# Retention, experts and a rational FFN in one program: moved row splits, output subtractions and first-group placement

## Chip, cores and metric

One core of one Trainium2 chip runs the whole program. The metric is the device time of one execution in microseconds (us); the figure for the kernel before is the median of three runs.

## What is computed

Three blocks follow each other, all in float32 precision. The first is attention with a decaying state, for 2 batches of 8 heads, 768 steps, head size 64. The second sends each of the 1536 tokens to one of 8 experts, in the order in which they come. The third is a feed-forward block with a rational function in the middle.

```python
state = gamma * state + k_t v_t^T;  y_t = scale * q_t state     # per head
logits = x @ w_gate;  expert_idx = argmax(logits);  gate_w = its softmax
h = relu(disp @ w1[e]);  y = h @ w2[e];  out = gate_w * y       # per expert
h = x @ w_in;  g = P(h) / (Q(h) + 1e-6);  return g @ w_out      # P, Q polynomials
```

## The kernel before

**Two parts for each float32 number.** TensorE (PE) multiplies in a rounded float32 format. So weights and activations are split into a rounded high part and a remainder, the low part, and a product is three matmuls: high by high, high by low, low by high. ScalarE (ACT) writes the high part (`whi`, `xh`, `yh`, ...) by a copy. VectorE (DVE) writes the low one by a subtraction (`wlo`, `xl`, `yl`, ...). Weights come in halves of 128 by 1024, six halves ahead of their use; `prep_next` (L169) loads one, splits the next one due, and stands once in every group of matmuls.

**Attention** goes over 12 units of 128 tokens. Of a unit, `scores` multiplies keys and queries, `mask` masks them on DVE, `inter` multiplies the state with the queries, `intra` adds the masked scores' products with the values, `attn_xt` scales the result on DVE, and `gate_mm` multiplies it with the gate weights of the experts one unit later. The values are first scaled by powers of gamma: by GpSimd (POOL) in `scale` (L275), up to unit 9. After units 0 to 6 (the first group) and 7 to 11 (the second) the tokens' places in the experts are worked out on DVE (`gate_parts`, `rank_pos`, `rank_put`, `gate_put`). In unit 10, `place_first` (L535) has PE add up the first group's places, DVE turns them into row indices, and POOL fetches by an indirect DMA the rows of expert 0's first 128 tokens into `xg0`. Those rows are transposed by PE in `early_x`, just after unit 11.

**Experts.** Expert 0 is done in two pieces, the first in the tail of attention, the second in `first_expert`, whose last result `y0` is transposed in expert 1 by `y_turn` (L848). Experts 1 to 7 run one loop (`moe`, L978). An expert has 224 token slots. Its up-projection is four groups (`fp`) of 24 matmuls into one of three PSUM banks `e1`; ACT takes the relu's high part `h` (L1006), DVE its remainder (L1007), and a weight half is split. In groups 1 and 3 `expert_x` (L963) transposes 128 or 96 rows of the next expert on PE and splits them into `xh` (ACT, L974) and `xl` (DVE, L975). All the transposed rows go through one PSUM bank, `xt`, so the next transposes wait for the `xl` before. Its down-projection is four quarters (`q`) of 16 matmuls into two PSUM tiles `acc[0]` and `acc[1]`, each the only buffer of its name. Of its four blocks `o` of 128 output columns, 0 and 1 go to `acc[0]`, 2 and 3 to `acc[1]`, and both tiles are written from the first quarter on: the order of the first matmuls is two pairs to `acc[0]`, then `acc[1]`.

At an expert's end `y_high` (L860) takes the high parts `yh` from both tiles on ACT, and `y_low` (L863) makes the remainders on DVE, two subtractions for each tile:

```python
tt(out=yl.bitcast(F32), in0=acc[:, :, 0], in1=yh.bitcast(F32), op=ALU.subtract)
tt(out=yl, in0=acc[:, :, 1], in1=yl.bitcast(F32), op=ALU.add)
```

**Beside this**, `dec_slot` decodes the feed-forward block's weights, which come as 64-bit numbers: in every third group or quarter two steps on ACT (L197, L198), in the next one two on DVE (L205, L206) and an addition on POOL (L209), then a store.

**What sets the order.** The program is written in the order in which each engine takes its instructions; nothing is moved by a scheduler. Each engine has its own queue and waits, by semaphores, for the others.

Of the kernel before, what the change touches and what calls it, by code (L numbers as in the profile page):

```python
# [21 lines left out]
E = 8  # L22
# [62 lines left out]
class Build:  # L85
# [528 lines left out]
    def attention(self):  # L614
        nc, tc, a = self.nc, self.tc, self.a
        with ExitStack() as st:
            self.ap = self.pool("attn", stack=st)
            self.pa = self.pool("pa", space=PSUM, stack=st)
            self.kv, self.sc, self.scm, self.s, self.yt, self.xt = {}, {}, {}, {}, {}, {}
            self.route, self.place, self.xk, self.rk, self.where = {}, {}, {}, {}, {}  # L620
            self.qd, self.yp = {}, {}
            n0, n1 = self.cols["ident"][0], self.cols["tri"][0]
            nk = self.cols["gk"][0]
            self.c0 = self.ap.tile([128, -(-(nk + H * D) // 32) * 32], F32, name="c0")[:, 0 : nk + H * D]
            self.ca = self.ap.tile([128, -(-(n0 - nk) // 32) * 32], F32, name="ca")[:, 0 : n0 - nk]
            self.wi = self.ap.tile([128, 4, 256], F32, name="wi")[:, :, 0:136]
            self.tri = self.ap.tile([128, 128], BF16, name="tri")
            self.ones = self.ap.tile([128, 128], BF16, name="ones")
            self.lgs = self.ap.tile([128, NU, 4, E], F32, name="lgs")
            self.xg0 = self.ap.tile([128, DM], F32, name="xg0")  # L630
            self.x0 = [self.ap.tile([128, 4, 128], F32R, name=n) for n in ("xh0", "xl0")]
            self.wu = self.ap.tile([128, 128], BF16, name="wu")
            self.attn_load(0, 0)
            nc.sync.dma_start(out=self.c0, in_=a["c0"])
            self.attn_load(1, 0)
            self.attn_part(0, 3)
            self.attn_load(1, 1)
            self.attn_load(2, 0)
            nc.sync.dma_start(out=self.ca[:, 0 : n1 - nk], in_=a["ct"][:, nk:n1])
            nc.sync.dma_start(out=self.ct, in_=a["ct"][:, n0:])  # L640
            self.attn_load(2, 1)
            for c in range(2):
                self.attn_load(3, c)
            nc.sync.dma_start(out=self.ca[:, n1 - nk :], in_=a["ct"][:, n1:n0])
            dve, pool = nc.vector, nc.gpsimd
            dve.memset(self.wu, 0.0)
            dve.memset(self.ones, 1.0)
            self.warm(WA)
            self.scores(0)
            self.mask_first()  # L650
            for h in (0, 4):
                self.scale(0, pool, slice(h, h + 4))
            self.y_table(0, pool)
            self.scale(1, pool)
            self.y_table(1, pool)
            self.warm(WC)
            ident = self.col("ident").unsqueeze(1).to_broadcast([128, 4, 128])
            wg = self.col("wg").rearrange("p (k e) -> p k e", e=E)
            done = {GROUPS[b + 1] - 1: b for b in range(len(GROUPS) - 1)}
            for u in range(NU):  # L660
                last = u == NU - 1
                if u + 4 < NU:
                    for c in range(2):
                        self.attn_load(u + 4, c)
                self.load_next(LOADS[u])
                if u + 2 < UA + 3:
                    self.scale(u + 2, pool)
                if u + 2 < UPB:
                    self.y_table(u + 2, pool)
                for n in LO_AT.get(u, ()):  # L670
                    self.split_lo(n // 2, n % 2)
                if 3 < u < NU - 1:
                    self.scores(u + 1)
                    self.mask(u + 1)
                if u - 2 in done:
                    next(gate)
                self.inter(u)
                if u - 4 in done:
                    self.place_first()
                if u == 3:  # L680
                    self.scores(u + 1)
                    self.mask(u + 1)
                self.intra(u)
                if u:
                    self.attn_xt(u)
                if u - 2 in done:
                    next(gate)
                if u:
                    self.state(u)
                if u < 3:  # L690
                    self.scores(u + 1)
                    self.mask(u + 1, 1 if u else 2)
                if u == 0:
                    self.state(u)
                if u == 0:
                    self.attn_xt(0)
                    nc.scalar.activation(out=self.wi[:, :, 0:128], in_=ident, func=AF.Copy)
                    nc.scalar.activation(out=self.wi[:, :, 128:], in_=wg, func=AF.Copy)
                if u == 3:
                    nc.scalar.activation(out=self.tri, in_=self.col("tri"), func=AF.Copy)  # L700
                    nc.scalar.activation(out=self.b0a, in_=self.ab[:, 4:5], func=AF.Abs)
                    nc.scalar.activation(out=self.b1a, in_=self.ab[:, 5:6], func=AF.Abs)
                    nc.vector.memset(self.cq, 1.0 + 1e-6)
                if u:
                    self.gate_mm(u - 1)
                if u - 2 in done and not last:
                    self.rank_mm(done[u - 2])
                if 0 < u < NU - 1:
                    self.gate_out(u - 1, (0,))
                for n in LO_MID.get(u, ()):  # L710
                    self.split_lo(n // 2, n % 2)
                if u - 1 in done:
                    gate = self.gate_parts(done[u - 1])
                    next(gate)
                if 0 < u < NU - 1:
                    self.gate_out(u - 1, (1,))
                if UA + 3 <= u + 2 < NU:
                    self.scale_heads(u + 2)
                for n in HI_AT.get(u, ()):
                    self.split_hi(n // 2, n % 2)  # L720
                if u - 2 in done and not last:
                    self.rank_pos(done[u - 2])
                if u - 3 in done and not last:
                    self.rank_put(done[u - 3])
                    self.gate_put(done[u - 3])
                for n in LO_END.get(u, ()):
                    self.split_lo(n // 2, n % 2)
            self.attn_tail()
# [250 lines left out]
    def moe(self):  # L979
        nc = self.nc  # L980
        with ExitStack() as st:
# [5 lines left out]
            mp = self.mp  # L987
            self.xh, self.xl = {}, {}
            self.first_expert()
            for e in range(1, E):  # L990
                xh, xl = (t.pop(e)[:, :, 0:W] for t in (self.xh, self.xl))
                h = {}
                for fp in range(4):
# [3 lines left out]
                    for fi in range(2):  # L997
# [9 lines left out]
                    nc.vector.scalar_tensor_tensor(  # L1007
                        out=hl, in0=ps, scalar=0.0, in1=hh.bitcast(F32), op0=ALU.max, op1=ALU.subtract
                    )
                    self.prep_next()  # L1010
                    if fp == 2 and e + 1 < E:
                        self.x_gate(e + 1, 1)
                    if fp % 2 and e + 1 < E:
                        self.expert_x(e + 1, fp // 2)
                        if e + 2 < E:
                            self.gather(2 * (e + 2) + fp // 2)
                    self.dec_slot(8 * e + fp)
# [4 lines left out]
                for q in range(4):  # L1022
# [14 lines left out]
                    if q == 3:  # L1037
                        at = bass.ds(self.start(e), W)
                        y = [(acc[i], slice(2 * i, 2 * i + 2), at) for i in range(2)]
                        for t in y:  # L1040
                            self.y_high(*t)
                            if e < E - 1:
                                self.y_low(*t)
                    if (e, q) == (1, 0):
                        self.y_turn(self.y0, 1)
                    if q == 2 and e + 2 < E:
                        self.x_gate(e + 2, 0)
# [375 lines left out]
```

## Time and profile before

| | |
|---|---|
| median of 3 runs | 507.47 us (507.04 to 509.14) |
| the profiled execution | 507.05 us |
| its span, first to last instruction | 505.3 us |
| PE busy | 494.8 us |
| DVE busy | 413.3 us |
| ACT busy | 365.9 us |
| POOL busy | 242.7 us |

The span runs from the first instruction of the program to the last. Attention takes about the first 55 us of it, the experts go on to about 246 us, and the feed-forward block takes the rest. Matmuls are pipelined: a row's duration is longer than the distance from its start to the next one's. A row of the timeline gives start, duration, engine, line, operation and tiles; the time in brackets is the engine's idle time before it and what ended that.

### The profile page before, as it was taken

The page shows a single profiled execution, that of the slowest core. Times are in us where ns is not written, and L with a number is a line of the kernel's source. Part 1 is how long each engine was busy: PE and PEld are TensorE (multiplying, and loading weights), DVE is VectorE, ACT ScalarE, POOL GpSimd, SP SyncE. Part 2 cuts the span into 40 slices and gives each one's busy share as a digit, 9 for nine tenths or more (in the row PEclk, how much of TensorE's full clock was granted, in tenths as well). Part 3 has the DMA queues.
Part 4 walks back from the last instruction along what each step waited for, and adds up shares of the span by engine and source line. Part 5 has one row for each costly group of instructions (what it writes and reads, how often), then busy time and mean ns, then how long its engine had stood idle before and what let it go on. Part 6 is the DMA issues. An engine that isn't in the chain of part 4 may idle for free.

```text
span 505.3 us, 9192 instructions
## 1 busy us (share of the span) xinstructions
PE 494.8 (98%) x3401; PEld 430.2 (85%) x3401; DVE 413.3 (82%) x602; ACT 365.9 (72%) x605; POOL 242.7 (48%) x187
## 2 busy tenths in 40 slices
PE   8999999999999999999999999999999999999995
PEld 5898878899999999898888888888888888888883
DVE  2579858789998987995696989999899998865973
ACT  1356639768677686755788989989999987767760
POOL 2621041033244734353464456767478774454774
PEclk9999999999999999999999999999999999999998
DMA  8999676898997999982400011312124000000203
GB/s 303 409 414 399 207 230 206 346 322 275 299 344 252 366 260 304 288 266 74 167 0 2 1 42 43 109 57 86 42 62 129 19 1 0 2 1 0 84 21 146
DMA packets 27265, 83.07 MB, mean 164 GB/s; under 512 B 4944, under 2 KB 5200, under 8 KB 27216
## 3 DMA queue, kind: packets, MB, share of 16 engines
q1 hardware_dynamic: 24160, 73.52, 42.4%
q0 software_dynamic: 2624, 7.35, 4.2%
q10 hardware_dynamic: 432, 1.57, 0.9%
q8 instruction: 27, 0.44, 0.3%
q14 instruction: 22, 0.18, 0.1%
HBM read 71.94 MB, written 10.49 MB: 163 GB/s over the span
## 4 chain that ended last, share of the span: by engine, by line
PE 64%; DVE 2%; issue 1%; ACT 1%; POOL 1%; POOLq 0%; DVEq 0%
PE h L1127 9%; PE h L1125 9%; PE h L1126 9%; PE acc L373 8%; PE o L1198 8%; PE o L1196 8%; PE o L1197 8%; PE e L1001 3%; PE e L1002 2%; PE e L1003 2%; POOL out L1227 1%; PE tp L971 0%; DVE wlo L154 0%; DVE fw L1162 0%; DVE fx L1164 0%
## 5 line engine op out<-in xcount | busy, mean ns | idle before, releaser
L154 DVE TENSOR_TENSOR wlo<-raw,whi 128x1024 fp32r<-128x1024 f32 x80 | 112.2, 1415 | 15.0 <-ACT whi L149 14.5
L1176 POOL TENSOR_TENSOR gg<-fx,gg 128x512 fp32r<-128x512 f32 x47 | 61.1, 1299 | 69.9 <-issue 62.1
L149 ACT ACTIVATE whi<-raw 128x1024 fp32r<-128x1024 f32 x80 | 83.5, 1054 | 1.8 <-PE acc L373 1.6
L1125 PE MATMUL h<-yh,whi 128*128 128x512 f32 x192 | 74.8, 390 | 0.0
L1196 PE MATMUL o<-whi,gg 128*128 128x512 f32 x192 | 74.8, 390 | 0.0
L1127 PE MATMUL h<-yh,wlo 128*128 128x512 f32 x192 | 74.8, 390 | 0.0
L1197 PE MATMUL o<-wlo,gg 128*128 128x512 f32 x192 | 74.7, 389 | 0.0
L1126 PE MATMUL h<-yl,whi 128*128 128x512 f32 x192 | 74.7, 389 | 0.0
L1198 PE MATMUL o<-whi,gg 128*128 128x512 f32 x192 | 74.7, 389 | 0.0
L373 PE MATMUL acc<-h,whi 128*128 128x448 f32 x224 | 71.4, 377 | 0.0
L1151 POOL TENSOR_TENSOR fw<-fh,fw 128x512 f32<-128x512 f32 x48 | 64.3, 1339 | 13.5 <-ACT fw L1140 12.8
L209 POOL TENSOR_TENSOR gq<-gq 128x512 int32<-128x512 int32 x16 | 26.1, 1628 | 86.0 <-DVE gq L206 47.9
L1138 ACT ACTIVATE fx<-h,ct 128x512 f32<-128x512 f32 x48 | 37.2, 776 | 37.6 <-PE h L1127 37.5
L1001 PE MATMUL e<-xh,whi 128*128 128x224 f32 x224 | 62.0, 277 | 0.1
L1002 PE MATMUL e<-xl,whi 128*128 128x224 f32 x224 | 61.5, 274 | 0.0
L1003 PE MATMUL e<-xh,wlo 128*128 128x224 f32 x224 | 61.5, 274 | 0.0
L373 PE MATMUL acc<-h,wlo 128*128 128x224 f32 x224 | 59.0, 263 | 0.0
L373 PEld LDWEIGHTS acc<-h,whi 128*128 128x128 f32 x224 | 42.0, 187 | 3.2
L1001 PEld LDWEIGHTS e<-xh,whi 128*128 128x128 f32 x224 | 43.0, 192 | 0.5 <-ACT yh L861 0.4
L1002 PEld LDWEIGHTS e<-xl,whi 128*128 128x128 f32 x224 | 43.0, 192 | 0.0
L1003 PEld LDWEIGHTS e<-xh,wlo 128*128 128x128 f32 x224 | 43.0, 192 | 0.0
L373 PEld LDWEIGHTS acc<-h,wlo 128*128 128x128 f32 x224 | 42.7, 191 | 0.1
(167 smaller groups left out, 1096.3 us busy)
## 6 DMA issues: line engine op xcount, KB each, us to landing
raw<-wm SPq DMA_DIRECT2D x61, 512.0 KB, 7.2
r<-wf SPq DMA_DIRECT2D x32, 512.0 KB, 4.9
kv<-kv SPq DMA_DIRECT2D x23, 512.0 KB, 8.5
wd<-gq SPq DMA_DIRECT2D x16, 256.0 KB, 6.6
raw<-wd SPq DMA_DIRECT2D x8, 512.0 KB, 6.7
xd<-xs SPq DMA_DIRECT2D x12, 256.0 KB, 7.1
raw<-wm ACTq DMA_DIRECT2D x3, 512.0 KB, 6.2
c<-c SPq DMA_DIRECT2D x1, 348.0 KB, 3.7
```

The costliest lines, as they stand in the source:

```text
L149: nc.scalar.activation(out=self.whi[i][:, sl], in_=raw, func=AF.Copy)
L154: (eng or self.nc.vector).tensor_tensor(out=self.wlo[i][:, sl], in0=raw, in1=self.whi[i][:, sl].bitcast(F32), op=ALU.subtract)
L373: self.nc.tensor.matmul(out, lhsT=w, rhs=x, start=start, stop=stop, skip_group_check=True)
L1001: nc.tensor.matmul(ps[:, fi], lhsT=wh[:, sl], rhs=xh[:, k], start=(k == 0), stop=False)
L1002: nc.tensor.matmul(ps[:, fi], lhsT=wh[:, sl], rhs=xl[:, k], start=False, stop=False)
L1003: nc.tensor.matmul(ps[:, fi], lhsT=wl[:, sl], rhs=xh[:, k], start=False, stop=(k == 3))
L1125: nc.tensor.matmul(h, lhsT=wh[:, sl], rhs=self.yh[:, k, ts], start=(k == 0), stop=False)
L1126: nc.tensor.matmul(h, lhsT=wh[:, sl], rhs=self.yl[:, k, ts], start=False, stop=False)
L1127: nc.tensor.matmul(h, lhsT=wl[:, sl], rhs=self.yh[:, k, ts], start=False, stop=(k == 3))
L1196: self.nc.tensor.matmul(ps, lhsT=gh[:, ms], rhs=wh[:, ws], start=first, stop=False)
L1197: self.nc.tensor.matmul(ps, lhsT=gh[:, ms], rhs=wl[:, ws], start=False, stop=False)
L1198: self.nc.tensor.matmul(ps, lhsT=gl[:, ms], rhs=wh[:, ws], start=False, stop=last)
```

## The change

Four places change in the order of the program; no arithmetic does.

- The scaling of unit 1's values on POOL is done in two halves of four heads.
- `place_first` in unit 10 stands behind `intra` and `attn_xt` of that unit, and no longer ahead of them.
- In groups 1 and 3 of an expert, `expert_x` stands ahead of the group's weight half. POOL's `gather` of the rows for the expert after next stays behind it.
- The `y_low` of an expert's two tiles stand in the next expert, one in group 0 and one in group 2, each behind that group's weight half. For expert 7 they stay at the end. `y_turn` of expert 0's last rows comes after the second quarter of expert 1's down-projection, and no longer after the first.

```diff
--- before.py
+++ after.py
@@ -651,7 +651,8 @@
             for h in (0, 4):
                 self.scale(0, pool, slice(h, h + 4))
             self.y_table(0, pool)
-            self.scale(1, pool)
+            for h in (0, 4):
+                self.scale(1, pool, slice(h, h + 4))
             self.y_table(1, pool)
             self.warm(WC)
             ident = self.col("ident").unsqueeze(1).to_broadcast([128, 4, 128])
@@ -675,14 +676,14 @@
                 if u - 2 in done:
                     next(gate)
                 self.inter(u)
-                if u - 4 in done:
-                    self.place_first()
                 if u == 3:
                     self.scores(u + 1)
                     self.mask(u + 1)
                 self.intra(u)
                 if u:
                     self.attn_xt(u)
+                if u - 4 in done:
+                    self.place_first()
                 if u - 2 in done:
                     next(gate)
                 if u:
@@ -987,6 +988,7 @@
             mp = self.mp
             self.xh, self.xl = {}, {}
             self.first_expert()
+            y = []
             for e in range(1, E):
                 xh, xl = (t.pop(e)[:, :, 0:W] for t in (self.xh, self.xl))
                 h = {}
@@ -1007,11 +1009,14 @@
                     nc.vector.scalar_tensor_tensor(
                         out=hl, in0=ps, scalar=0.0, in1=hh.bitcast(F32), op0=ALU.max, op1=ALU.subtract
                     )
+                    if fp % 2 and e + 1 < E:
+                        self.expert_x(e + 1, fp // 2)
                     self.prep_next()
                     if fp == 2 and e + 1 < E:
                         self.x_gate(e + 1, 1)
+                    if fp % 2 == 0 and y:
+                        self.y_low(*y.pop(0))
                     if fp % 2 and e + 1 < E:
-                        self.expert_x(e + 1, fp // 2)
                         if e + 2 < E:
                             self.gather(2 * (e + 2) + fp // 2)
                     self.dec_slot(8 * e + fp)
@@ -1039,9 +1044,7 @@
                         y = [(acc[i], slice(2 * i, 2 * i + 2), at) for i in range(2)]
                         for t in y:
                             self.y_high(*t)
-                            if e < E - 1:
-                                self.y_low(*t)
-                    if (e, q) == (1, 0):
+                    if (e, q) == (1, 1):
                         self.y_turn(self.y0, 1)
                     if q == 2 and e + 2 < E:
                         self.x_gate(e + 2, 0)
```

On DVE, between the down-projection of expert 1 and the second group of expert 2, there stood (`yl` are the subtractions of `y_low`, each with a register instruction, ISA; `h` a group's remainder; `wlo` a weight half):

```order
L870 TENSOR_LOAD st_83
L865 ISA
L865 TENSOR_TENSOR yl<-acc,yh 128x2x224
L866 ISA
L866 TENSOR_TENSOR yl<-acc,yl 128x2x224
L865 ISA
L865 TENSOR_TENSOR yl<-acc,yh 128x2x224
L866 ISA
L866 TENSOR_TENSOR yl<-acc,yl 128x2x224
L1007 SCALAR_TENSOR_TENSOR h<-e_1614,h 128x2x224
L154 TENSOR_TENSOR wlo<-raw,whi 128x1024
L1007 SCALAR_TENSOR_TENSOR h<-e_1652,h 128x2x224
```

and with the change, over the same place:

```order
L871 TENSOR_LOAD st_83
L1009 SCALAR_TENSOR_TENSOR h<-e_1611,h 128x2x224
L154 TENSOR_TENSOR wlo<-raw,whi 128x1024
L866 ISA
L866 TENSOR_TENSOR yl<-acc,yh 128x2x224
L867 ISA
L867 TENSOR_TENSOR yl<-acc,yl 128x2x224
L1009 SCALAR_TENSOR_TENSOR h<-e_1651,h 128x2x224
```

The four subtractions ahead of the first remainder are gone; the first two stand behind the first weight half.

On DVE, from the remainder of group 1 of expert 2 to that of group 3 (`xl` the next expert's rows; `gq` the decoder), there stood:

```order
L1007 SCALAR_TENSOR_TENSOR h<-e_1652,h 128x2x224
L154 TENSOR_TENSOR wlo<-raw,whi 128x1024
L975 TENSOR_TENSOR xl<-tp,xh 128x4x128
L205 TENSOR_SCALAR gq<-gq 128x512
L206 SCALAR_TENSOR_TENSOR gq<-r_1530,gq 128x512
L1007 SCALAR_TENSOR_TENSOR h<-e_1700,h 128x2x224
L154 TENSOR_TENSOR wlo<-raw,whi 128x1024
L1007 SCALAR_TENSOR_TENSOR h<-e_1737,h 128x2x224
L154 TENSOR_TENSOR wlo<-raw,whi 128x1024
```

and with the change:

```order
L1009 SCALAR_TENSOR_TENSOR h<-e_1651,h 128x2x224
L976 TENSOR_TENSOR xl<-tp,xh 128x4x128
L154 TENSOR_TENSOR wlo<-raw,whi 128x1024
L205 TENSOR_SCALAR gq<-gq 128x512
L206 SCALAR_TENSOR_TENSOR gq<-r_1520,gq 128x512
L1009 SCALAR_TENSOR_TENSOR h<-e_1699,h 128x2x224
L154 TENSOR_TENSOR wlo<-raw,whi 128x1024
L866 ISA
L866 TENSOR_TENSOR yl<-acc,yh 128x2x224
L867 ISA
L867 TENSOR_TENSOR yl<-acc,yl 128x2x224
L1009 SCALAR_TENSOR_TENSOR h<-e_1738,h 128x2x224
```

The rows' `xl` moved ahead of the weight half, and the other two subtractions came in behind group 2's weight half, ahead of group 3's remainder.

On PE, in unit 10 (`yt<-kv,s` is `inter`, `yt<-scm,kv` is `intra`, `tp` and `L540` are the place matmuls):

```order
 L373 MATMUL sc<-kv 128x128 x8
 L373 MATMUL yt<-kv,s 64x128 x8
+L373 MATMUL yt<-scm,kv 64x128 x8
 L533 MATMUL tp<-rr,pe 128x96 x7
 L540 LDWEIGHTS ones
 L540 MATMUL tp<-run,ones 128x1
-L373 MATMUL yt<-scm,kv 64x128 x8
 L373 MATMUL st<-kv 64x64 x8
 L373 MATMUL xk<-wi,xt 64x136 x8
```

The unit's value products moved ahead of the place matmuls.

## Rows read from the trace of the kernel before

**Rows 1.** The page: its first line, and the busy time of the engines (share of the span).
```profile
span 505.3 us, 9192 instructions
...
PE 494.8 (98%) x3401; PEld 430.2 (85%) x3401; DVE 413.3 (82%) x602; ACT 365.9 (72%) x605; POOL 242.7 (48%) x187
```

**Rows 2.** Waits of PE over the whole span: us in total, times, longest.
```profile
PE ytp L852 <- DVE xl L975: 1.1, 1, 1.1
...
PE tp L971 <- DVE xl L975: 0.9, 1, 0.9
...
PE tp L533 <- DVE rr L527: 0.3, 1, 0.3
...
PE yt L373 <- POOL kv L278: 0.3, 1, 0.3
```

**Rows 3.** Expert 5 as one stretch: us, busy per engine, PEclk, DMA share, GB/s.
```profile
172.19:193.80 21.61, 21.61 (x170) 21.14 (x169) 19.11 (x23) 13.95 (x21) 12.18 (x9) 1.00 1.02 296
```

**Rows 4.** Timeline of POOL in unit 1: start us, us, what, [idle before it].
```profile
9.82 1.04 POOL L278 TENSOR_TENSOR kv<-kv,c 128x512 f32<-128x512 f32 x1 [3.69 <-DMA kv<-kv]
```

**Rows 5.** Timeline of DVE in unit 10, same columns.
```profile
50.94 0.69 DVE L381 TENSOR_TENSOR xt<-yt,qd 128x512 f32<-128x512 f32 x1 [0.21 <-PE yt L373]
```

**Rows 6.** POOL's gather in unit 10: its timeline row, and its time to landing by source line.
```profile
50.34 1.20 POOL L921 DMA_INDIRECT xg<-xd,gidx  x1 [10.59 <-DVE tab L544]
...
DMA to landing us min/median/max: 3.6/3.6/3.6
```

**Rows 7.** Timeline of PE: first-group transposes; first matmuls into `acc[1]`, experts 2, 4, 5, 7.
```profile
54.76 0.44 PE L735 MATMUL xtp<-ct,xg 128*128 128x128 f32 x2
...
119.17 0.38 PE L373 MATMUL acc<-h,whi 128*128 128x448 f32 x1
...
162.78 0.38 PE L373 MATMUL acc<-h,whi 128*128 128x448 f32 x1
...
184.40 0.37 PE L373 MATMUL acc<-h,whi 128*128 128x448 f32 x1
...
227.82 0.37 PE L373 MATMUL acc<-h,whi 128*128 128x448 f32 x1
```

**Rows 8.** Timeline of DVE in expert 2.
```profile
107.10 0.62 DVE L865 TENSOR_TENSOR yl<-acc,yh 128x448 f32 x1 [0.35 <-ACT yh L861]
...
110.41 0.62 DVE L1007 SCALAR_TENSOR_TENSOR h<-e,h 128x448 fp32r<-128x448 f32 x1 [0.84 <-ACT h L1006]
...
111.36 1.22 DVE L154 TENSOR_TENSOR wlo<-raw,whi 128x1024 fp32r<-128x1024 f32 x1 [0.33 <-ACT whi L149]
...
114.04 1.23 DVE L154 TENSOR_TENSOR wlo<-raw,whi 128x1024 fp32r<-128x1024 f32 x1 [0.32 <-ACT whi L149]
...
115.18 0.68 DVE L975 TENSOR_TENSOR xl<-tp,xh 128x512 fp32r<-128x512 f32 x1
...
115.78 0.42 DVE L205 TENSOR_SCALAR gq<-gq 128x512 int32<-128x512 int32 x1
...
116.23 0.69 DVE L206 SCALAR_TENSOR_TENSOR gq<-r,gq 128x512 int32<-128x512 int32 x1
...
116.84 0.62 DVE L1007 SCALAR_TENSOR_TENSOR h<-e,h 128x448 fp32r<-128x448 f32 x1
...
117.37 2.16 DVE L154 TENSOR_TENSOR wlo<-raw,whi 128x1024 fp32r<-128x1024 f32 x1
```

**Rows 9.** Timeline of POOL in expert 2.
```profile
117.16 1.28 POOL L209 TENSOR_TENSOR gq<-gq 128x512 int32<-128x512 int32 x1 [8.10 <-ACT whi L149]
```

**Rows 10.** Timeline of DVE in experts 4 and 5.
```profile
154.42 0.62 DVE L1007 SCALAR_TENSOR_TENSOR h<-e,h 128x448 fp32r<-128x448 f32 x1 [1.20 <-ACT h L1006]
...
182.62 2.15 DVE L154 TENSOR_TENSOR wlo<-raw,whi 128x1024 fp32r<-128x1024 f32 x1
```

**Rows 11.** Timeline of ScalarE (ACT) in experts 2 and 7.
```profile
116.06 1.05 ACT L149 ACTIVATE whi<-raw 128x1024 fp32r<-128x1024 f32 x1
...
219.88 0.54 ACT L1006 ACTIVATE h<-e 128x448 fp32r<-128x448 f32 x1
```


## Prediction

> **What bounds the kernel now.** I read the page's busy times first, then the waits of TensorE (PE), then its trace stage by stage, and last VectorE's (DVE's) order in the expert stage. PE is busy 494.8 us of a span of 505.3 [rows 1], and the view of its waits lists little between start and tail [rows 2]: 1.1 us for the transposes of `y_turn`, 0.9 us for a set of transposes in `expert_x`, 0.3 us for the place matmuls of unit 10, 0.3 us for GpSimd's (POOL's) scaling of unit 1. So PE bounds the kernel, and an edit counts only by what it takes from PE's waits or adds to them. DVE is the engine to watch. In expert 5 it is busy 19.11 us of 21.61, at a granted clock of 1.00 [rows 3], and its queue is in order: what is put ahead of an instruction that PE needs makes it late by its whole length.
>
> **Attention, the two small edits.** The scaling of unit 1 takes 1.04 us in one piece [rows 4]. In two halves the first is ready after about 0.5, heads 0 to 3 can start without PE's 0.3 us of waiting, and the second half is ready about when PE gets to it. I take 0.3 us; the ends are 0 (the next thing is late by as much) and 0.4.
>
> Placing the first group behind unit 10's value products removes PE's other wait of 0.3 us. But three things now stand later: the place matmuls, behind the products; the index computation on DVE, behind `attn_xt(10)` (0.69 us) where it was ahead of it [rows 5]; and the gather on POOL, issued at 50.34, which lands 3.6 us after its issue [rows 6] and whose rows PE transposes at 54.76 [rows 7]. So they landed some 0.8 us before PE used them. PE now comes 0.3 us sooner and the rows about 0.6 later, and the margin is used up. I take nothing; the ends are a gain of 0.3 and a loss of 0.3.
>
> **Experts, what is removed.** `y_turn` comes a quarter later, and `expert_x` ahead of the weight half, so that `xl` is not behind a subtraction of 1.2 us: PE's wait of 1.1 us goes. In expert 6 the transposes waited 0.9 us [rows 2] for an `xl` that stood behind the four subtractions of `y_low` at the expert's start; that goes too. Together 2.0 us.
>
> **Experts, what is added.** `y_low` reads the down-projection's accumulators, two PSUM tiles with one buffer each. Until now all four of its subtractions ran right after an expert's last matmul, half an expert before PE wrote these tiles again. Now the second pair, that of `acc[1]`, stands behind the third up group's remainder **and** its weight half. PE's fifth matmul of the down-projection writes `acc[1]` and must wait for that pair, and all of PE's queue behind it. The wait is new, in experts 2 to 7.
>
> I walk expert 2 with the starts of DVE's rows [rows 8], PE's times kept. A row's successor starts about 0.08 before its end (114.04 + 1.23, then 115.18). The weight half of group 0 starts at 111.36. Behind it, at 112.50, goes the first `y_low` pair, twice 0.62, so 1.20 to the next start. Then group 1's remainder (0.62) is at 113.70, `xl` at 114.24, its weight half at 114.84, the decoder's two steps at 115.98 and 116.43, group 2's remainder at 117.04. The decoder's POOL addition starts 0.24 after the second step ends (116.92, then 117.16) and takes 1.28 [rows 9]. In the trace the weight half behind it starts at 117.37, takes 2.16 and ends 1.09 after POOL; alone it takes 1.22. So here POOL runs from 117.36 to 118.64, the half ends at 119.73, and the second pair, 1.28 long, at 120.93. PE wants `acc[1]` at 119.17 [rows 7]. **Wait: 1.8 us.**
>
> The others by the same steps:
> - Expert 5 has the decoder in the same place: 1.8. In the trace its third weight half runs from 182.62 to 184.77 [rows 10], already past PE's 184.40, before any `y_low` is put behind it.
> - Expert 3 has no decoder step ahead. The weight half waits for its high part from ScalarE, which in expert 2's times ends at 117.11 [rows 11]: half 117.15 to 118.37, pair to 119.57, wait 0.45 with the signal. This is the least that any of experts 2 to 6 can have.
> - Expert 4 has the decoder after the first pair. From group 0's remainder at 154.42 [rows 10], with 0.95 to its half as at 110.41 to 111.36: pair 156.51, decoder 157.71, remainder 158.77, `xl` 159.31, POOL 159.09 to 160.37, half to 161.46, group 2's half 161.92 to 163.14, second pair to 164.34, against 162.78: 1.6.
> - Expert 6 has the decoder ahead of group 0, where POOL delays the first half by about a microsecond: 1.2, between 0.8 and 1.5 by when ScalarE has the decoder's input.
> - Expert 7 has shorter up groups and no transposes. ScalarE frees group 0 at 220.42 [rows 11]: remainder 220.45, half 221.40, pair 222.54, decoder 223.74, remainder 224.80, POOL to 226.40, half to 227.49, next half to 229.17, pair to 230.37, against 227.82: 2.6, taken as 2.4 since that ScalarE step moves up a little.
>
> Sum 1.8 + 0.45 + 1.6 + 1.8 + 1.2 + 2.4 = 9.25. DVE's own work does not grow, and behind the wait it has room again: the last group's remainder is needed only when three quarters of the down-projection are done, and `xl` only at the next expert. So I cost what is queued behind the second pair at nothing; were that cover gone, the next expert's first group would wait.
>
> **A rule beside it.** The row shows that a weight half started beside POOL's addition takes 2.16 instead of 1.22. The Trainium skill (SBUF — State Buffer, Who interferes with whom) says that a DVE instruction with two SBUF inputs and a GpSimd instruction that reads SBUF exclude each other, and that issue order decides which waits. By that rule, the trace agrees (2.16 against 1.22), and the price falls on DVE wherever a step that reads PSUM stands between decoder and half; were POOL the one to wait, the time would be the second rival's.
>
> **Sum.** 507.05 (the profiled run: span 505.3 and 1.75 around it) + 9.25 − 2.0 − 0.3 = 514.0. The median of the runs is 0.42 above the profiled one, less than my terms are sure to.
>
> **Rivals.**
> - *The second pair is in time* (faster): PE never waits on `acc[1]`, and 507.05 − 2.3 = 504.75. It decides in expert 2 at 119.17: DVE must have ended the third half by 117.9. For it: none of DVE's work grew. Against: ScalarE alone ends that half's high part at 117.11, and the half takes 1.22. 5%.
> - *The halves win against POOL*: where the decoder is near, a wait is shorter by up to 0.94: 0.9, 0.45, 1.3, 0.9, 0.5, 1.5, sum 5.55, so 507.05 + 5.55 − 2.3 = 510.3. For it: a few tenths decide which starts first. Against: rows 8, where POOL did, with the same order. 20%.
> - *It balances*: all six waits as small as expert 3's, 2.7 against 2.3: 507.45. Rows 10 speak against it (expert 5). 9%.
> - *It piles up*: a late decoder step holds up loads and ScalarE, every expert pays 0.6 more, and the gather is late too: 507.05 + 12.85 − 2.0 = 517.9. 14%.
>
> **Numbers.** The forecast itself has 52%. The range is 509.8 to 517.5: from just under the second rival to just under the last. A measurement tells about 0.5% (2.5 us) from no change. Slower by more: forecast, second and last rival, 86%; within: 9%; faster: 5%.
>
> **What would show it.** PE's waits must list `acc` waiting for DVE's `yl` (the second subtraction), six times, longest in expert 7, 7 to 11 us in all; `ytp` and `tp` waiting for `xl` must be gone, and the wait for POOL's `kv` nearly so. If `xtp` waits for the gather, the margin was smaller than read. The prediction is wrong if no `acc` waits for `yl`, or if the sum of these waits is under 5 us.

## The result and the profile after

The changed kernel takes 513.89 us (median of 4 runs, 513.38 to 515.21), the kernel before 507.62 beside it. The ratio is 1.0123, 95% interval 1.0093 to 1.0152: slower by 1.2%. The forecast was 514.0, range 509.8 to 517.5. The profiled execution took 514.13 us; the figures below compare it with the profiled 507.05 of before.

The changed kernel's page, its first line and its busy times, which answer to [rows 1]:

```profile
span 512.3 us, 9187 instructions
...
PE 496.0 (97%) x3401; PEld 429.7 (84%) x3401; DVE 409.3 (80%) x602; ACT 366.5 (72%) x605; POOL 242.4 (47%) x188
```

PE's busy time grew by 1.2 us (its rows' modelled ends) and the span by 7.0. DVE works no longer than before; PE stands still for longer. Its waits over the span, which answer to [rows 2] (us in total, times, longest):

```profile
PE acc L373 <- DVE yl L867: 6.7, 6, 1.9
PE sc L373 <- DMA kv<-kv: 1.1, 1, 1.1
PE wp L302 <- DVE wu L646: 1.0, 1, 1.0
PE yt L373 <- ACT s L344: 0.5, 1, 0.5
PE xtp L736 <- DMA xg<-xd,gidx: 0.5, 1, 0.5
```

The waits of `ytp` and `tp` for `xl`, those for `rr` and for POOL's `kv` are gone. A new one stands at the top: `acc` for the second subtraction of `y_low`, six times. Three of the six on PE's timeline, with the rows around the first (start us, us, engine, line, operation; in brackets the idle time before and what ended it):

```profile
118.59 0.38 PE L373 MATMUL acc<-h,whi 128*128 128x448 f32 x1
118.81 0.27 PE L373 MATMUL acc<-h,wlo 128*128 128x224 f32 x1
119.75 0.47 PE L373 MATMUL acc<-h,whi 128*128 128x448 f32 x1 [0.68 <-DVE yl L867]
120.06 0.26 PE L373 MATMUL acc<-h,wlo 128*128 128x224 f32 x1
120.16 0.38 PE L373 MATMUL acc<-h,whi 128*128 128x448 f32 x1
...
166.03 0.47 PE L373 MATMUL acc<-h,whi 128*128 128x448 f32 x1 [1.85 <-DVE yl L867]
...
234.71 0.47 PE L373 MATMUL acc<-h,whi 128*128 128x448 f32 x1 [1.92 <-DVE yl L867]
```

These are the first matmuls into `acc[1]`, as in [rows 7]. A wait costs more than its bracket says. Between the starts of 118.81 and 119.75 lie 0.94 us where 0.10 is usual, as from 120.06 to 120.16; and the first matmul behind the wait takes 0.31 to the next start, where another takes 0.21 or 0.22. That is 0.94 in all for a bracket of 0.68. PE's weight loads (PEld) show it too: the load of the matmul at 120.16 started 0.10 ahead of it, at 120.06, but that of the matmul behind the wait only together with it:

```profile
119.75 0.19 PEld L373 LDWEIGHTS acc<-h,whi 128*128 128x128 f32 x1 [0.96 <-DVE yl L867]
120.06 0.19 PEld L373 LDWEIGHTS acc<-h,whi 128*128 128x128 f32 x1
```

So the time is counted by the starts of the experts' first matmuls in the two traces. The row of expert 7 ends at the first matmul of the feed-forward block, which comes behind the first quarter of that expert's down-projection:

| stretch | before, us | after, us | difference | bracket of `acc` | forecast |
|---|---|---|---|---|---|
| start to expert 1 | 83.67 | 84.72 | +1.05 | | -0.3 |
| expert 1 | 23.28 | 21.97 | -1.31 | | -1.1 |
| expert 2 | 21.61 | 22.56 | +0.95 | 0.68 | +1.8 |
| expert 3 | 21.94 | 22.49 | +0.55 | 0.30 | +0.45 |
| expert 4 | 21.69 | 23.79 | +2.10 | 1.85 | +1.6 |
| expert 5 | 21.61 | 23.56 | +1.95 | 1.67 | +1.8 |
| expert 6 | 22.67 | 22.19 | -0.48 | 0.30 | +1.2 - 0.9 |
| expert 7 | 13.23 | 15.41 | +2.18 | 1.92 | +2.4 |
| the rest | 275.58 | 275.64 | +0.06 | | 0 |

The waits add 8.28 (expert 6's wait of before was worth 1.03 by distance), the removed ones give 2.34 (1.31 and 1.03), the start takes 1.05; with 0.06 that is 7.05. Between the medians the loss is 6.3.

### The profile page after: what moved, and what is told of

Its sections match the earlier page's. It is cut to its first block, busy times and chain, and to the rows that moved or that the text cites. A ratio compares the mean times of both kernels' runs of the same rounds, so it can differ in the third digit from the quotient of the medians.

```text
span 512.3 us, 9187 instructions
## 1 busy us (share of the span) xinstructions
PE 496.0 (97%) x3401; PEld 429.7 (84%) x3401; DVE 409.3 (80%) x602; ACT 366.5 (72%) x605; POOL 242.4 (47%) x188
## 4 chain that ended last, share of the span: by engine, by line
PE 57%; DVE 6%; issue 3%; ACT 2%; POOL 1%; POOLq 0%; DVEq 0%; ACTq 0%
PE h L1128 9%; PE h L1130 9%; PE h L1129 8%; PE acc L373 8%; PE o L1199 7%; PE o L1201 7%; PE o L1200 7%; DVE wlo L154 2%; ACT whi L149 1%; DVE yl L866 1%; POOL out L1230 1%; DVE yl L867 1%; DVE h L1009 1%; PE e L1005 1%; PE e L1004 1%
## 5 line engine op out<-in xcount | busy, mean ns | idle before, releaser
L154 DVE TENSOR_TENSOR wlo<-raw,whi 128x1024 fp32r<-128x1024 f32 x80 | 107.9, 1363 | 13.3 <-ACT whi L149 13.0
```

The costliest lines, as they stand in the source:

```text
L154: (eng or self.nc.vector).tensor_tensor(out=self.wlo[i][:, sl], in0=raw, in1=self.whi[i][:, sl].bitcast(F32), op=ALU.subtract)
```

## The experiments

The letters stand for the theories named in the expectations. "W" is the forecast's: `acc[1]` has one buffer, its second pair of subtractions comes too late, and PE waits. All ratios are to the kernel before, run beside them.

**Is the late pair the loss?** First all four subtractions go back to the expert's end; the other moves stay (`low_end`):

```diff
-                    if fp % 2 == 0 and y:
-                        self.y_low(*y.pop(0))
...
                             self.y_high(*t)
+                            if e < E - 1:
+                                self.y_low(*t)
```

> The changed kernel with one part undone: all four subtractions of y_low stand at the expert's end again; the other moves stay. Theory W (PE waits for acc[1]'s late pair, and that is the whole loss): no matmul of acc waits for yl, and the distance that the six waits added, 8.3 us by the starts of experts 2 to 7 in the changed kernel's trace, goes: 513.9 - 8.3 = 505.6 us, between 505 and 506.5. Rival O (the loss lies in the other moves: xl ahead of the weight half, or the first group's placement): the time stays above 510.

Measured: 505.47 us, ratio 0.9966 (0.9949 to 0.9984). No matmul of `acc` waits. The whole loss goes, and what is left of the change is a gain of 0.3%. O, that the other moves cost the time, is out.

Then the kernel before with that move alone (`low_only`).

> The kernel before with one part of the change alone: y_low in groups 0 and 2 of the next expert, each behind the weight half. W: six waits of acc for yl come back, the wait of expert 6's transposes (1.0 by distance) goes, that of y_turn (1.3) stays: 507.6 + 8.3 - 1.0 = 514.9 us, between 513.5 and 516. O: within 2.5 us of the kernel before, 507.6.

Measured: 517.45 us, ratio 1.0194 (1.0158 to 1.023), 2.5 us more than expected and above the range. The six waits are there (7.3 us), but two experts take longer than in the changed kernel: expert 2 by 0.94, as its wait is 1.61 and not 0.68 (the race behind this is told under the attention edits), and expert 4 by 2.28, with 26.07 us. The table by stretches shows why expert 4 does (us, then busy us of PE, its weight loads, DVE, ACT, POOL, each with a count, then the granted clock, DMA share, GB/s):

```profile
164.00:167.00 3.00, 1.96 (x15) 1.50 (x13) 3.00 (x5) 3.00 (x7) 2.70 (x2) 1.00 0.99 270
167.00:168.30 1.30, 0.00 (x0) 0.00 (x1) 1.27 (x4) 1.30 (x3) 0.92 (x1) 1.00 0.87 251
168.30:170.00 1.70, 1.70 (x6) 1.57 (x7) 1.70 (x3) 0.64 (x1) 0.00 (x0) 0.55 0.98 375
170.00:171.60 1.60, 1.60 (x7) 1.51 (x6) 1.57 (x4) 0.26 (x1) 0.00 (x0) 0.50 1.05 428
171.60:174.00 2.40, 2.40 (x16) 2.25 (x16) 2.40 (x2) 1.01 (x2) 2.17 (x2) 0.94 0.97 362
```

PE stood still for 0.83 us before the transposes at 165.53 and for 1.51 before `acc[1]` at 168.30. Right behind the second stop the granted clock is 0.50, the lower of its two levels, for more than 3 us. In that stretch the first matmul of a pair takes 0.40 to the next start, not 0.21:

```profile
170.09 0.60 PE L373 MATMUL acc<-h,whi 128*128 128x448 f32 x1
170.49 0.39 PE L373 MATMUL acc<-h,wlo 128*128 128x224 f32 x1
```

Of the 2.28 us the transposes' wait is 0.83, the shorter `acc` wait -0.34, and the 1.8 that are left go with the lower clock. The mechanism is W's; the clock is a price that W had left out.

Third, DVE's order stays as changed and PE's demand is moved (`acc_late`): in the first two quarters the matmuls into `acc[0]` come first, then those into `acc[1]`.

```diff
-                    for f in range(2 * q, 2 * q + 2):
+                    fs, os = (range(4), range(2 * q, 2 * q + 2)) if q < 2 else (range(2 * q, 2 * q + 2), range(4))
+                    for f in fs:
                         x = h[f // 2][:, f % 2]
-                        for o in range(4):
+                        for o in os:
```

> The changed kernel, DVE's order untouched, with PE's demand moved instead: the first two quarters of a down-projection do all their matmuls into acc[0] first (eight pairs), then those into acc[1], so that acc[1] is first written 6 pairs of 0.315 us, 1.9 us, later. W (the single buffer of acc[1] is what PE waits for): the six waits, at most 1.92 us, shrink to 0.1 or nothing: 513.9 - 8.3 = 505.6 us, between 505 and 507. Rival D (DVE is too slow as a whole in these experts, and PE waits for it wherever it stands): a new wait of a similar size further on in the same expert, 510 or more.

Measured: 506.82 us, ratio 0.9986 (0.9971 to 1.0002), 1.2 above the expectation and within its range. With the subtractions in the same place, the loss goes: what counts is when PE wants the buffer. PE's waits:

```profile
PE tp L972 <- ACT xg L962: 0.8, 1, 0.8
PE acc L373 <- DVE yl L867: 0.7, 1, 0.7
PE xtp L736 <- DMA xg<-xd,gidx: 0.7, 1, 0.7
```

Five of the six waits are gone. The one of 0.7 is expert 4's, where DVE's first remainder comes 5.1 us behind the expert's first matmul (154.29 and 149.20; 4.3 in the changed kernel's expert 4, 156.08 and 151.74). The wait of `tp` is no heir of `acc`'s: `xl` is ready, ACT's scaling of the rows (`x_gate`) is late (see below). So D, that DVE is too slow wherever PE waits for it, is out but for expert 4.

The changed kernel was run a second time beside these (`again`).

> The changed kernel once more, beside the others: 513.9 us, between 513 and 514.8; acc waiting for yl six times, 6 to 8 us in all, longest in experts 4, 5 and 7 (1.6 to 2.0 each), shorter in 2, and 0.3 in 3 and 6. The place where it may differ is expert 2, where POOL's addition and the third weight half start within 0.2 us of each other: 0.7 with the half first, up to 1.7 with POOL first.

Measured: 513.46 us, ratio 1.0125 (1.0099 to 1.015). The waits repeat: 0.68, 0.30, 1.80, 1.69, 0.30, 1.92.

**Where may the second pair stand?** In group 2, but ahead of the weight half (`pair_first`):

```diff
+                    if fp == 2 and y:
+                        self.y_low(*y.pop(0))
                     self.prep_next()
...
-                    if fp % 2 == 0 and y:
+                    if fp == 0 and y:
```

> The changed kernel with the second pair of y_low ahead of group 2's weight half, no longer behind it. W with the half as the length that matters: by the changed kernel's DVE rows the pair would end at 118.6, 140.3, 164.8, 187.5, 209.6 and 233.5 in experts 2 to 7, PE wants acc[1] at 119.1, 141.6, 164.2, 187.9, 211.5 and 232.8, so 0.7 us of wait each is left in experts 4 and 7 and none elsewhere: 513.9 - 8.3 + 1.4 = 507.0 us, between 506 and 508.5. Rival G (any place in group 2 is too late, since the third group's remainder alone comes too late): waits in four experts or more, over 510.

In group 1, behind its half (`low_fp1`): `if fp < 2 and y` in place of `if fp % 2 == 0 and y`.

> The changed kernel with the second pair of y_low in group 1 of the next expert, behind its xl and its weight half, no longer in group 2. W: by the changed kernel's rows the pair would end at 164.3 in expert 4 and 233.0 in expert 7, where PE wants acc[1] at 164.2 and 232.8; two waits of 0.1 to 0.2 us are left and none elsewhere: the time of the kernel with all four subtractions at the end, 505.5, and 0.4: 505.9 us, between 505 and 507. Rival G (a subtraction inside the next expert only passes the lateness on, to group 2's remainder and the next transposes): new waits of tp or e, 508 or more.

Measured: `pair_first` 508.55 us, 1.0035 (1.0011 to 1.0059); `low_fp1` 508.39, 1.0036 (1.0009 to 1.0064). Both get back about 5 us of the loss, neither reaches the kernel with the pair at the end, and both lie above their expected ranges (506 to 508.5 and 505 to 507). The waits of `acc`, of `pair_first` first, then of `low_fp1`, with its other new one:

```profile
PE acc L373 <- DVE yl L867: 1.7, 2, 0.9
```

```profile
PE tp L972 <- ACT xg L962: 1.4, 1, 1.4
...
PE acc L373 <- DVE yl L867: 0.9, 1, 0.9
```

In `pair_first` waits remain in experts 4 (0.84) and 7 (0.89) and nowhere else, as expected with 0.7 each: the weight half ahead of the pair is the length that decides, and G of `pair_first` (waits in four experts or more) is out in this execution. In `low_fp1` expert 7 keeps 0.88 where 0.2 was expected, and its time and its new wait of `tp` are what the G of that run named. That wait is for ACT's `x_gate` and not for DVE, and `x_turn` below has it without a late pair; but G isn't excluded for `low_fp1`. The runs of both spread widely (507.0 to 512.5 and 506.5 to 514.1). The profiled execution of `pair_first` is its shortest, that of `low_fp1` (507.98) among the shorter ones, so what the longer ones waited for is open.

**What is POOL's part?** The decoder's addition is left out (`no_add`).

> The changed kernel without the decoder's addition on POOL (16 additions are left out, so the low parts of the feed-forward weights are missing). W with POOL as the reason of the long halves: no half behind a decoder step takes more than 1.25 us; the wait in expert 4 is 0.3 shorter, in 5 by 0.9, in 7 by 0.95, in 2, 3 and 6 as before: 513.9 - 2.2 = 511.7 us, between 511 and 512.8. Rival S (the long halves don't set the waits, or have another cause): 513.9, within 0.6.

Measured: 523.2 us, ratio 1.0301 (1.0269 to 1.0333): slower by 9 us where 2 less were expected. It answered another question. The addition waits for DVE, and so paces POOL's queue; without it the scatters of row numbers behind it follow each other at once, eight from 167.89 to 179.36, where the changed kernel has three before its next addition. ACT's waits from 160 to 200:

```profile
ACT gq L197 <- DMA wd<-gq: 12.1, 3, 5.7
ACT h L1009 <- PE e L1006: 2.2, 1, 2.2
```

ACT's decoder step waits 12.1 us for stores that free its buffers. The three stores issued from 165 to 185 land 14.3 us after their issue (median), where the one store of the changed kernel whose landing its trace gives took 6.7. That the bunched scatters hold the stores up is likely, but no run shows it alone. All of ACT's queue stands behind the decoder step, and PE then waits 3.9 us for `x_gate`, with its clock at 0.50 from 198 to 202 and not at 1.00 again before 204. Its total can't tell W from S, that the long halves don't set the waits.

So the addition was kept and only shortened from 512 columns to 16 (`short_add`):

```diff
-        nc.gpsimd.tensor_tensor(out=out, in0=g, in1=q, op=ALU.add)
+        nc.gpsimd.tensor_tensor(out=out[:, 0:w], in0=g[:, 0:w], in1=q[:, 0:w], op=ALU.add)
...
-        self.dec_dve(n, g)
+        self.dec_dve(n, g, 16)
```

> The changed kernel with the decoder's addition on POOL cut from 512 columns to 16 (the other columns of the feed-forward weights' low parts are missing): POOL still waits for DVE there and still stands in the same order, but no longer works beside a weight half for 1.3 us. W with POOL as the reason of the long halves: every half of DVE takes 1.25 us or less, the wait in expert 4 is shorter by 0.3, in 5 by 0.9, in 7 by 0.95, the others as they were: 513.9 - 2.2 = 511.7 us, between 510.8 and 512.8. Rival S (the halves are long for another cause): 513.9, within 0.6, with halves of 2.15 us left.

Measured: 515.15 us, ratio 1.0145 (1.0122 to 1.0169): the total misses both theories, and of the three parts two hit. Its timeline of DVE's halves and POOL:

```profile
116.90 1.21 DVE L154 TENSOR_TENSOR wlo<-raw,whi 128x1024 fp32r<-128x1024 f32 x1
117.07 1.12 POOL L209 TENSOR_TENSOR gq<-gq 128x16 int32<-128x16 int32 x1 [8.33 <-DVE h L1009]
...
160.39 0.22 POOL L209 TENSOR_TENSOR gq<-gq 128x16 int32<-128x16 int32 x1 [11.17 <-DVE gq L206]
...
161.21 1.22 DVE L154 TENSOR_TENSOR wlo<-raw,whi 128x1024 fp32r<-128x1024 f32 x1
...
233.00 0.21 POOL L209 TENSOR_TENSOR gq<-gq 128x16 int32<-128x16 int32 x1 [8.00 <-DVE gq L206]
233.21 1.21 DVE L154 TENSOR_TENSOR wlo<-raw,whi 128x1024 fp32r<-128x1024 f32 x1
```

No half takes 2 us any more. Expert 4 waits 1.55 and expert 7 0.96, against 1.85 and 1.92 in the changed kernel: shorter by 0.30 and 0.96, where 0.3 and 0.95 were expected. Expert 5's wait is the miss: 1.91, against 1.67, where 0.9 less was expected. There the transposes wait 0.93 for an `x_gate` that ACT, held up for 2.7 us by a store, does late, and PE's clock is at 0.50 from 190 to 196, so that the expert takes 27.85 us in place of 23.56. This execution is the longest of its six. S is out for the halves, and for the waits of experts 4 and 7.

**The two attention edits**, both undone (`no_att`), then the scaling alone (`scale_one`).

> The changed kernel without its two attention edits (one-piece scaling of unit 1, first group's placement ahead of unit 10's value products). W with attention at -0.3: 0.3 us slower than the changed kernel run beside it; with the gather late as the changed kernel's trace shows (0.46): within 0.3 either way. Rival A (the attention edits cost the 1.05 us that separate the two profiled executions at expert 1's start): 0.8 to 1.1 us faster than the changed kernel beside it. As it has y_low late and xl ahead of the half, expert 4's transposes don't wait, and PE's clock stays at its upper level in expert 4, other than with y_low alone moved (0.50 to 0.61 for about 3.5 us).

> The changed kernel with one edit undone: the scaling of unit 1 in one piece again. Theory R (the one POOL instruction more moves POOL's later work, and so decides the race in expert 2): POOL's addition in expert 2 starts 0.24 us behind DVE's second decoder step, not 0.62, and ahead of the third weight half, which takes 2.15 us; the wait for acc[1] in expert 2 is 1.6 us, not 0.7; the others as before. With 0.3 for unit 1's own wait: 513.5 + 0.9 + 0.3 = 514.7 us, between 513.8 and 516. Rival A (the first group's placement decides it): wait in expert 2 of 0.7 as in the changed kernel, 513.8 or less.

Measured: `no_att` 515.91 us (1.0165, 1.0137 to 1.0193) and `scale_one` 516.29 (1.0175, 1.0149 to 1.0201), against ratios of 1.0123 and 1.0125 of the changed kernel. Both lie above what was expected: `no_att` by 2 us, `scale_one` just over its range. A (the two edits cost a microsecond; or the placement, not the scaling, decides the race) is out in both. R, by which the scaling decides a race in expert 2, shows in expert 2 of `scale_one`:

```profile
115.30 0.69 DVE L206 SCALAR_TENSOR_TENSOR gq<-r,gq 128x512 int32<-128x512 int32 x1
116.24 1.28 POOL L209 TENSOR_TENSOR gq<-gq 128x512 int32<-128x512 int32 x1 [6.89 <-ACT whi L149]
116.44 2.15 DVE L154 TENSOR_TENSOR wlo<-raw,whi 128x1024 fp32r<-128x1024 f32 x1
...
119.16 0.62 DVE L866 TENSOR_TENSOR yl<-acc,yl 128x448 f32 x1
```

against the changed kernel, with expert 6's group 0 and expert 7 below:

```profile
116.15 0.69 DVE L206 SCALAR_TENSOR_TENSOR gq<-r,gq 128x512 int32<-128x512 int32 x1
117.29 1.22 DVE L154 TENSOR_TENSOR wlo<-raw,whi 128x1024 fp32r<-128x1024 f32 x1
117.46 2.18 POOL L209 TENSOR_TENSOR gq<-gq 128x512 int32<-128x512 int32 x1 [7.27 <-ACT xg L962]
...
119.07 0.62 DVE L867 TENSOR_TENSOR yl<-acc,yl 128x448 f32 x1
...
201.06 1.28 POOL L209 TENSOR_TENSOR gq<-gq 128x512 int32<-128x512 int32 x1 [1.66 <-DVE gq L206]
...
203.51 1.23 DVE L154 TENSOR_TENSOR wlo<-raw,whi 128x1024 fp32r<-128x1024 f32 x1 [0.33 <-ACT whi L149]
...
229.41 1.30 POOL L209 TENSOR_TENSOR gq<-gq 128x512 int32<-128x512 int32 x1 [6.46 <-DVE gq L206]
229.62 2.17 DVE L154 TENSOR_TENSOR wlo<-raw,whi 128x1024 fp32r<-128x1024 f32 x1
...
232.25 1.21 DVE L154 TENSOR_TENSOR wlo<-raw,whi 128x1024 fp32r<-128x1024 f32 x1
...
234.03 0.62 DVE L867 TENSOR_TENSOR yl<-acc,yl 128x448 f32 x1
```

POOL's addition starts 0.25 behind the end of DVE's second decoder step in `scale_one`, ahead of the half, and 0.62 behind it in the changed kernel, after the half. Whoever starts first runs at its own length, the other ends some 1.1 us after the first has: half 2.15 behind POOL, addition 2.18 behind the half. The Trainium skill (SBUF — State Buffer, Who interferes with whom) says that issue order decides which of the two is held up, and the traces agree. In expert 2 the wait is 1.61 in `scale_one` and 0.68 in the changed kernel; in `no_att`, which has the scaling in one piece too, it is 1.62. The second cost is the clock, in `scale_one` behind the waits of experts 4 and 7; here expert 7's:

```profile
236.00:238.00 2.00, 1.59 (x10) 1.51 (x11) 2.00 (x4) 0.36 (x1) 0.02 (x1) 0.99 0.83 306
238.00:240.00 2.00, 2.00 (x7) 1.73 (x6) 1.16 (x2) 0.00 (x0) 0.00 (x0) 0.50 0.01 4
240.00:242.00 2.00, 2.00 (x7) 1.55 (x6) 0.00 (x0) 0.00 (x0) 0.00 (x0) 0.66 0.00 0
```

and the same place in the changed kernel, 2 us earlier:

```profile
236.00:238.00 2.00, 2.00 (x12) 1.76 (x11) 1.45 (x2) 0.00 (x0) 0.00 (x0) 1.00 0.05 17
```

It cost 1.63 us in expert 4 (25.42 against 23.79, with waits of 1.88 and 1.85) and 1.6 behind expert 7's wait, 1.25 of it in the feed-forward block's start. In `no_att` the clock stays at 1.00 in expert 4, as expected, and falls to 0.50 behind expert 7's wait. Expert 2's wait and the clock are what both runs had more than expected. Runs of `no_att` and `scale_one` whose mean clock was 0.998 or more took 514.05 to 515.29; those below 0.993 took 517.3 to 517.7. Expert 1 starts in these and the other traces between 83.4 and 84.2 us without the placement and scaling edits (4 executions), 83.7 to 84.7 with both (8): no gain that can be told, and a loss of no more than some tenths.

**What is good in the change?** `expert_x` ahead and `y_turn` later alone (`x_turn`, with all else as before); then these with the split scaling (`best`).

> The kernel before with two parts of the change alone: expert_x ahead of the weight half in groups 1 and 3, and y_turn a quarter later; both attention edits and y_low as before. W: the waits of y_turn and of expert 6's transposes go (2.3 us by the starts of experts) and nothing else changes: 507.1 (the last median of the kernel before) - 2.3 = 504.8 us, between 504.2 and 505.6. Rival H (a weight half behind xl makes the next group's PE work late, so that a new wait takes back half or more): 506 or more.

> The changed kernel with y_low back at the expert's end and the first group's placement back ahead of unit 10's value products; so the parts kept are the split scaling, expert_x ahead and y_turn later. W: PE has no wait of over 0.2 us behind the first 11 us except that for rr (0.3), none for the gather: 504.7 us, between 504 and 505.6, so at least as fast as the kernel with all four subtractions at the end (505.5). Rival P (the placement behind the products saves 0.3 net): 505.8 or more.

Measured: `x_turn` 505.34 us, 0.9962 (0.995 to 0.9974); `best` 505.43, 0.9974 (0.9962 to 0.9986). Both lie within their ranges, H's 506 and P's 505.8 were not reached. With `low_end` three versions are faster than the kernel before, by 0.3 to 0.4%, and can't be told apart. `best` has the shortest profiled span, 503.2 us, and its list of PE's waits names none in the experts:

```profile
PE wp L302 <- DVE wu L646: 1.0, 1, 1.0
PE yt L373 <- ACT s L344: 0.5, 1, 0.5
PE tp L533 <- DVE rr L527: 0.3, 1, 0.3
```

The profiled execution of `x_turn` is its longest (507.34). PE's transposes wait twice there for `x_gate`, 0.87 and 0.84; ahead of each, an ACT step of the decoder had waited, 2.7 and 1.3 us, for the store of an earlier one, and ACT's rows follow each other without a gap from there to the late `x_gate`. The same wait stands ahead of the late `x_gate` of `low_fp1` (1.8) and `acc_late` (1.3). ACT waits for such stores in the kernel before as well (0.9 to 3.5), without making PE's transposes late. No run here removed these waits, so whether the weight half's new place (H) favours the late `x_gate` is open.

## Why the prediction was right, point by point

- **What bounds, and the new wait:** right. DVE's work did not grow, PE's waits list `acc` for `yl` six times, the longest in expert 7; their 6.7 us lie just under the 7 to 11 named. `low_end`, `acc_late` and `low_only` show it from three sides.
- **Experts 3, 4, 5:** 0.45, 1.6 and 1.8 forecast; brackets 0.30, 1.85, 1.67. The walk by DVE's rows holds to 0.25.
- **Expert 2:** 1.8 forecast, 0.68 found. The step that failed is "So here POOL runs from 117.36 to 118.64". POOL's addition started 0.62 behind the decoder's second step, not 0.24, and lost the race by 0.17. In `scale_one` and `no_att` the step holds, with 1.61 and 1.62. It is the rival *the halves win against POOL*, come true in one expert.
- **Expert 6:** 1.2 forecast, 0.30 found. "POOL delays the first half by about a microsecond" failed: the addition ended at 202.34, before the half began at 203.51. The four subtractions no longer stand ahead of the decoder step, and its input from ACT came sooner, as ACT waited 0.46 us for a store there and 3.53 in the kernel before. So nothing delays the half, and the wait is at expert 3's value, the least.
- **Expert 7:** 2.4 forecast, 1.92 found. Its half takes 2.17 behind POOL, as taken. The step that failed is the size of "since that ScalarE step moves up a little": ACT's relu of group 0 starts 2.88 behind the expert's first matmul (221.28), where the walk took 3.41 from the kernel before [rows 11]. That is 0.53 sooner, and the forecast had taken off 0.2.

```profile
224.16 0.55 ACT L1008 ACTIVATE h<-e 128x448 fp32r<-128x448 f32 x1 [0.98 <-PE e L1005]
```

- **What is removed:** 2.0 forecast from the brackets, 2.34 by distance. In the same way the six waits cost 8.28 by distance and 6.72 by brackets. The sum took brackets throughout.
- **Attention:** "the margin is used up" was right (`xtp` waits 0.3 to 1.0 us for the gather in six of the eight traces with the placement and the scaling changed). The -0.3 of the scaling is there at its own place, as PE's wait for unit 1's values (`kv`) is 0.2 to 0.5 in the five traces with one piece and absent in all with two, but the start of expert 1 doesn't come sooner for it. There the trace has +1.05, of which 0.64 is there already at unit 1, whose scores wait 1.12 for a late load of keys. The same wait is 0.8 and 1.1 in `low_only` and `x_turn`, which have no attention edit, and absent in `pair_first`, which has both: it is scatter, and the sum had no term for it.
- **The sum:** 6.95 forecast, 7.05 measured between the profiled executions. It is this close by luck, as errors cancel: brackets -2.5, distance +1.6, removed -0.3, attention and rest +1.4.

Of the rivals, *the second pair is in time* and *it balances* fell on six waits. *It piles up* didn't happen in the changed kernel, but its late decoder step stands ahead of what costs in `no_add` and the profiled `short_add`.

## What to carry to other kernels

Before work is moved away from a queue's head, ask who needs the buffer that it frees, and walk that engine's rows up to the time at which the buffer is written again; here four subtractions that looked idle at an expert's start held two PSUM tiles that PE wanted half an expert later. Price a stall of PE by the distance between starts, here about 0.25 us over the bracket each time, and ask whether the clock falls behind it. Try the parts of a change apart: here the moves of `expert_x` and `y_turn` gained 0.4%, the two in attention nothing that could be told, and the late subtractions cost 1.6% in the changed kernel.

## What was not expected of the hardware

- **One POOL instruction more in unit 1 decided a race 106 us later.** In expert 2 the addition starts 0.61 to 0.63 us behind DVE's second decoder step in all programs with the split scaling (the changed kernel, `again`, `low_end`, `best`, `low_fp1`, `acc_late`, `pair_first`, `short_add`), and 0.23 to 0.25 in those without (before, `low_only`, `x_turn`, `no_att`, `scale_one`). `best` and `x_turn` differ in nothing else. What holds POOL for 0.38 us there no run shows.
- **PE's clock fell behind waits of 1.5 to 1.9 us in some executions and not in others.** The changed kernel's waits in experts 4 and 7, 1.80 to 1.92, left it at 1.00 in both profiled executions; 1.88 and 1.90 in `scale_one` were followed by 0.50 for more than 3 us; and in the profiled execution of `no_att` 1.92 (expert 4) left it there and 1.91 (expert 7) didn't. What decides between them is open.
- **An addition of 16 columns takes 0.21 us, or 1.12 when a weight half has just begun.** One of 512 columns takes 1.28 and 2.18.
- **An addition that was thought to be in the way kept POOL's scatters apart:** `no_add`, without it, is 9 us slower than the changed kernel, with its stores landing late.
